# Attention and two expert layers on one core: the second low part of layer one moves from GpSimd to VectorE

## Chip, core and metric

One NeuronCore of a Trainium2 chip runs the whole program. The time is the device time of one execution in microseconds, lower is better; the number used is the median of several executions.

## What is computed

```
# decaying causal linear attention, blockwise: q, k, v [2, 8, 768, 64]
out[block] = ((q k^T) * Dmask) v + (q * lam_pow) kv_state
kv_state   = lam_block * kv_state + (k * rev_pow)^T v
# layer one: 1536 tokens x 512, one of 8 experts each (cosine logits, argmax)
out[mask] = gate * (relu(x[mask] @ w1[e]) @ w2[e])     # w1 [8, 512, 1024], w2 [8, 1024, 512]
# layer two: the same shapes, two of 8 experts each (noisy logits, top 2)
out[mask] += top2_w * (relu(x[mask] @ w1[e]) @ w2[e])
```

All of it is float32.

## The kernel before, in words

The attention runs first, in 12 tiles of 128 rows. Then the expert layers run as 18 **jobs**, one after the other: jobs 0 to 7 are the eight experts of layer one, with capacities of 224, 224, 224, 216, 208, 200, 192 and 184 tokens; jobs 8 to 17 belong to layer two. A job is 8 **steps**, one for each 128 hidden units, so there are 144 steps, numbered `s`. In a step TensorE makes the hidden units (`hstep`, tile `h` in PSUM) and, for the step two before (`LAG = 2`), the products with the second weight matrix (`ystep`, tiles `y`).

Float32 accuracy comes from splitting. `split(s)` is called three steps ahead (`LEAD = 3`) and cuts a weight tile into a high part in the format fp32r and a low part in bfloat16. For the first matrix ScalarE copies the high part `h1` (line 348) and VectorE subtracts to get the low part `l1` (line 350). For the second matrix ScalarE copies `h2` (line 349), and the low part `l2` (line 352) is subtracted by GpSimd or by VectorE, whichever the expression on line 352 chooses. Before, GpSimd does it as long as the job that step `s - 14` belongs to is one of layer one: for steps 0 to 77. From step 78 on VectorE does it. Steps 0 to 2 are split while the attention still runs. In 16 of the 144 steps nothing is split, so there are 128 `l2`.

The hidden units leave PSUM through ScalarE (`hs`, high part, line 778) and VectorE (`hs`, low part, line 779). Both engines work in order. So do the others, and the order of each is the order of the code: the dictionary `todo` says at which step which piece of the routing runs. The routing of layer two is computed job by job from the output of layer one (`gate_*`, `pe_0`, `pe_1`, `post1_*`, lines 840 to 1005): many small operations on VectorE, ScalarE and GpSimd, then gathers of token rows by GpSimd's DMA (line 693). Weights are reloaded by ScalarE's queue (lines 320 and 322); a reload waits until the subtractions have read the buffer.

Of the kernel before, what the change touches and what calls it, by code (L numbers as in the profile page):

```python
# [8 lines left out]
FT = mybir.dt.float32  # L9
# [20 lines left out]
NF = F // 128  # L30
# [25 lines left out]
LEAD = 3  # L56
# [8 lines left out]
XG6 = (6, 6, 6, 8, 8)  # L65
XG7 = (6, 6, 6, 7, 7)
C7 = (1, 1, 4)
POOL2 = 14
XP1 = (4, 6)
GATES = (-1, 1, 1, 2, 5, 6, 9)  # L70
GATES0 = (5, 5, 6, 7, 9, 8, 9)
# [28 lines left out]
def emit(ctx, tc, qt, kt, k, v, lam, moe_expert_emb, moe_tau, moe_w1, moe_w2, moe2_w_gate, moe2_w_noise,  # L100
         moe2_noise, moe2_w1, moe2_w2, out):
    nc = tc.nc
# [187 lines left out]
    JOBS = [Job(0, c, e=e) for e, c in enumerate(STAT1)]  # L290
# [37 lines left out]
    def drip(n=1):  # L328
        for _ in range(min(n, len(small))):
            fn, *a = small.pop(0)  # L330
            fn(*a)

    def split(s):
        if s >= NSTEP:
            return
        u, x = divmod(s, 4)
        r1, r2 = RAW[u]
        a1 = r1[:, :, x * 128:(x + 1) * 128]
        a2 = r2[:, x, :]
        if s % NF in JOBS[s // NF].raw:  # L340
            SPLIT[s] = (a1, None, a2, None)
            drip()
            return
        h1 = wts.tile([128, KD, 128], FR, name="h1", bufs=LEAD + 1)
        h2 = wts.tile([128, DM], FR, name="h2", bufs=LEAD + 2 + LAG)
        l1 = wts.tile([128, KD, 128], BF, name="l1", bufs=LEAD + 1)
        l2 = wts.tile([128, DM], BF, name="l2", bufs=LEAD + 2 + LAG)
        nc.scalar.activation(h1, a1, AF.Copy)  # L348
        nc.scalar.activation(h2, a2, AF.Copy)  # L349
        nc.vector.tensor_sub(l1, a1, h1.bitcast(FT))  # L350
        drip()
        (nc.gpsimd if not JOBS[max(0, s - POOL2) // NF].ly else nc.vector).tensor_sub(l2, a2, h2.bitcast(FT))  # L352
        SPLIT[s] = (h1, l1, h2, l2)


# [188 lines left out]
    for i in range(NTI + 1):  # L544
# [34 lines left out]
        if i in SPLITS:  # L579
            split(SPLITS.index(i))  # L580
# [53 lines left out]
    def parts(x):  # L634
        jb = JOBS[0]
        c = jb.c
        if not x:
# [6 lines left out]

    CALLS = {"E": early, "F": first_rows, "J": join, "P": parts, "O": O, "X": X, "R1": R1, "R2": R2,
             "RC": RC, "S": lambda i: split(len(SPLITS) + n - i), "W": lambda i: warm_up(WARM1[n - i], "px"), "R3": R3, "R4": R4}
    n = NTI - 1
    for calls in LATE:
# [583 lines left out]
    for u in range(3, 2 * NJ):  # L1232
        raw = [f % 4 for f in JOBS[(u - 3) // 2].raw if f // 4 == (u - 3) % 2]
        s = 4 * (u - 3) + max([WF] + [x + LAG for x in raw])
# [3 lines left out]
    for s in range(NSTEP + LAG):  # L1238
        j, f = divmod(s, NF)
        if s < NSTEP:  # L1240
            hstep(s)

        if s >= LAG and not (f == LAG and 0 < j <= E):
            if f == LAG + 1 and 0 < j <= E:
                ystep(s - LAG - 1)
            ystep(s - LAG)
        if f == LAG - 1 and j and not (j == NJ and JOBS[-1].row):
            ycopy(j - 1)
        for u in loads.get(s, ()):
            wload(u, nc.scalar)  # L1250
        if 12 <= s < 12 + 4 * 8 and s % 4 == 0:
            zero_out(s // 4 - 3)
        for fn, a in sorted(todo.get((j, f), ()), key=lambda x: (post1_e, pe_0, pe_1).index(x[0]) if x[0] in (post1_e, pe_0, pe_1) else 3):
            if fn in stages:
                drip(99)
            fn(*a)
        split(s + LEAD)
# [224 lines left out]
```

## Time and profile before

| | |
|---|---|
| median of 3 executions | 614.44 us (612.76 to 615.24) |
| the profiled execution | 615.32 us, span 613.6 us |
| TensorE matmul busy | 579.9 us, 95% of the span |
| VectorE busy | 395.1 us, 64% |
| ScalarE busy | 295.3 us, 48% |
| GpSimd busy | 303.2 us, 49% |
| granted TensorE clock, mean | 0.98 |

Busy means that an instruction of the engine is open in the trace, also while it waits inside for something. Matmuls are pipelined and their ends are modelled, so TensorE's busy share says little by itself; its idle times, and what ended them, say more. Attention takes the first 84 us, layer one from there to about 285 us, layer two the rest. All "us" in rows of the trace count from the start of the span.

### The profile page before, as it was taken

The numbers are of one execution on the slowest core, as the hardware profiler recorded it, in microseconds if no ns is written. First come the engines' busy times: TensorE is split into PE (matmuls) and PEld (weight loads), VectorE is DVE, ScalarE is ACT, GpSimd is POOL, SyncE is SP. The second block draws the span as 40 slices with busy tenths as digits, with TensorE's granted clock in tenths as the row PEclk, the third lists the DMA queues.
The fourth block names the chain that finished last, engine by engine and source line by source line (L and its number), as shares of the span: only waits on it lengthen the run. The fifth ranks groups of instructions, "written<-read, shape, count | busy, mean of one in ns | idle before, by whom it ended". The sixth has DMA issues, their size and how long they took to land.

```text
span 613.6 us, 11525 instructions
## 1 busy us (share of the span) xinstructions
PE 579.9 (95%) x4212; PEld 474.1 (77%) x4213; DVE 395.1 (64%) x1097; ACT 295.3 (48%) x689; POOL 303.2 (49%) x484
## 2 busy tenths in 40 slices
PE   5999889999988999998989999999999999999992
PEld 2898778888877888886766877777777898679761
DVE  3688847898898798898987447465664127323620
ACT  1466426776665667665444434344443135314410
POOL 5676547977867678776763500341303332412203
PEclk8899999999999999999999999999999999999996
DMA  7999546858866674675675732554526637737103
GB/s 202 342 332 391 226 131 208 300 201 297 285 222 242 235 268 173 232 251 173 207 212 209 226 139 63 126 196 154 107 93 171 209 71 234 257 138 189 18 5 56
DMA packets 59955, 119.52 MB, mean 195 GB/s; under 512 B 5469, under 2 KB 7045, under 8 KB 59890
## 3 DMA queue, kind: packets, MB, share of 16 engines
q10 hardware_dynamic: 37232, 73.74, 34.3%
q0 software_dynamic: 9376, 25.48, 16.3%
q1 hardware_dynamic: 13282, 19.48, 9.5%
q8 instruction: 35, 0.57, 0.4%
q14 instruction: 30, 0.25, 0.1%
HBM read 100.55 MB, written 18.14 MB: 193 GB/s over the span
## 4 chain that ended last, share of the span: by engine, by line
PE 79%; DVE 8%; POOL 4%; DMA 3%; issue 3%; ACT 1%; ACTq 0%; DVEq 0%; POOLq 0%
PE h L756 11%; PE h L757 10%; PE h L759 9%; PE y L759 7%; PE y L754 6%; PE y L757 4%; PE y L756 4%; PE t L732 3%; PE h L750 3%; PE y L750 3%; PE y L786 2%; PE y L787 2%; PE y L788 2%; PE po L410 2%; PE px L443 2%
## 5 line engine op out<-in xcount | busy, mean ns | idle before, releaser
L756 PE MATMUL h<-xs,h 128*128 128x224 f32 (+10 forms) x512 | 152.9, 322 | 4.2 <-DVE hs L779 4.2
L1050 POOL DMA_INDIRECT out_dram<-orow,ix x30 | 47.6, 1586 | 206.3 <-DVE orow L1048 153.0
L757 PE MATMUL h<-xs,h 128*128 128x224 f32 (+10 forms) x512 | 142.8, 302 | 0.3 <-DVE xs L737 0.3
L350 DVE TENSOR_TENSOR l<-r,h 128x512 bf16<-128x512 f32 x128 | 112.9, 882 | 35.3 <-ACT h L348 34.9
L352 POOL TENSOR_TENSOR l<-r,h 128x512 bf16<-128x512 f32 x78 | 103.6, 1336 | 15.5 <-ACT h L349 14.1
L759 PEld LDWEIGHTS <-l 128*128 128x128 bf16 x896 | 68.8, 97 | 45.5 <-issue 24.0
L778 ACT ACTIVATE hs<-h 128x224 fp32r<-128x224 f32 (+10 forms) x128 | 52.0, 406 | 105.5 <-PE h L759 97.0
L756 PEld LDWEIGHTS h<-xs,h 128*128 128x128 f32 x512 | 97.4, 190 | 6.9 <-DVE hs L779 5.1
L757 PEld LDWEIGHTS h<-xs,h 128*128 128x128 f32 x512 | 97.5, 190 | 1.8 <-DVE xs L737 1.0
L779 DVE SCALAR_TENSOR_TENSOR hs<-h,hs 128x224 fp32r<-128x224 f32 (+10 forms) x128 | 57.8, 452 | 54.0 <-ACT hs L778 53.0
L759 PE MATMUL h<-xs,l 128*128 128x224 bf16 (+10 forms) x512 | 87.4, 292 | 0.0
L348 ACT ACTIVATE h<-r 128x512 fp32r<-128x512 f32 x128 | 79.8, 623 | 9.9 <-POOL l L352 4.8
L349 ACT ACTIVATE h<-r 128x512 fp32r<-128x512 f32 x128 | 79.4, 621 | 0.0
L759 PE MATMUL y<-hs,l 128*128 128x224 bf16 (+8 forms) x384 | 70.3, 289 | 0.0
L754 PE MATMUL y<-hs,h 128*128 128x448 f32 (+5 forms) x256 | 68.0, 384 | 0.0
L737 DVE TENSOR_TENSOR xs<-t,xs 128x416 fp32r<-128x416 f32 (+7 forms) x42 | 24.6, 587 | 48.7 <-ACT xs L736 48.5
L756 PE MATMUL y<-hs,h 128*128 128x416 f32 (+2 forms) x128 | 51.2, 400 | 0.0
L736 ACT ACTIVATE xs<-t 128x416 fp32r<-128x416 f32 (+7 forms) x42 | 21.5, 516 | 53.5 <-PE t L732 48.2
L788 PE MATMUL y<-h,hs 128*128 128x512 f32 x80 | 46.6, 583 | 0.0
L757 PE MATMUL y<-hs,h 128*128 128x416 f32 (+2 forms) x128 | 44.7, 349 | 0.0
L754 PEld LDWEIGHTS y<-hs,h 128*128 128x128 f32 x256 | 44.0, 191 | 0.9
L693 POOL DMA_INDIRECT xw<-x,g x28 | 30.9, 1103 | 15.0 <-PE h L759 7.3
(274 smaller groups left out, 987.6 us busy)
## 6 DMA issues: line engine op xcount, KB each, us to landing
r<-in_moe_w_dram ACTq DMA_DIRECT2D x66, 1024.0 KB, 8.3
r<-in_moe_w_dram SPq DMA_DIRECT2D x6, 1024.0 KB, 9.1
x<-row POOLq DMA_DIRECT2D x8, 517.0 KB, 5.3
out_dram<-zeros ACTq DMA_DIRECT2D x7, 512.0 KB, 6.4
qt<-in_qt_dram SPq DMA_DIRECT2D x12, 256.0 KB, 5.8
kr<-in_k_dram SPq DMA_DIRECT2D x12, 256.0 KB, 7.9
vt<-in_v_dram SPq DMA_DIRECT2D x12, 256.0 KB
x<-xr POOLq DMA_DIRECT2D x11, 265.0 KB, 3.8
```

The lines of the kernel that those rows point to most:

```text
L348: nc.scalar.activation(h1, a1, AF.Copy)
L349: nc.scalar.activation(h2, a2, AF.Copy)
L350: nc.vector.tensor_sub(l1, a1, h1.bitcast(FT))
L352: (nc.gpsimd if not JOBS[max(0, s - POOL2) // NF].ly else nc.vector).tensor_sub(l2, a2, h2.bitcast(FT))
L754: nc.tensor.matmul(o[:, :2 * c], hi, mov, start=first, stop=False, skip_group_check=True)
L756: nc.tensor.matmul(o[:, :c], hi, mov[:, :c], start=first, stop=False, skip_group_check=True)
L757: nc.tensor.matmul(o[:, :c], hi, mov[:, c:], start=False, stop=False, skip_group_check=True)
L759: nc.tensor.matmul(o[:, :c], lo, upper_half(mov[:, :c]), start=False, stop=last, skip_group_check=True)
L778: nc.scalar.activation(hh, ph[:, :c], AF.Relu)
L779: nc.vector.scalar_tensor_tensor(hl, ph[:, :c], 0.0, hh.bitcast(FT), op0=OP.max, op1=OP.subtract)
L788: nc.tensor.matmul(PY[j][t], hl, h2, start=False, stop=f == NF - 1)
L1050: s = nc.gpsimd.indirect_dma_start(out=out[:, :], out_offset=bass.IndirectOffsetOnAxis(ap=ix[:p, t:t + 1], axis=0), in_=row[:p], in_offset ...
```

## The change

`l2` goes to GpSimd for the three steps that are split during the attention, and to VectorE for all others. The arithmetic, the buffers and the rest of the code stay as they are.

```
-POOL2 = 14
...
         nc.scalar.activation(h1, a1, AF.Copy)
         nc.scalar.activation(h2, a2, AF.Copy)
         nc.vector.tensor_sub(l1, a1, h1.bitcast(FT))
         drip()
-        (nc.gpsimd if not JOBS[max(0, s - POOL2) // NF].ly else nc.vector).tensor_sub(l2, a2, h2.bitcast(FT))
+        (nc.gpsimd if s < LEAD else nc.vector).tensor_sub(l2, a2, h2.bitcast(FT))
         SPLIT[s] = (h1, l1, h2, l2)
```

75 instructions move, one for each of the steps 3 to 77. A line was taken out at the top of the file, so that every later line has a number one lower after the change. TensorE's, ScalarE's and SyncE's instructions keep their order. The weights `l2` on TensorE and the weight reloads of ScalarE's queue now wait for VectorE where they waited for GpSimd.

On VectorE, the place is the fifth step of job 3, where the routing of an earlier job makes the tables `pa` and `pb`. Before:

```order
L993 TENSOR_TENSOR pa_2671<-iotap,r2s 128x512
L995 TENSOR_TENSOR ge_2601<-ge_2601 128x4x12
L996 TENSOR_TENSOR pb_2672<-oi_2605,ge_2601 128x384
L350 TENSOR_TENSOR l_2685<-r_2178,h_2683 128x512
L779 SCALAR_TENSOR_TENSOR hs<-h,hs 128x216
L737 TENSOR_TENSOR xs<-t,xs 128x2x208
L350 TENSOR_TENSOR l_2725<-r_2178,h_2723 128x512
L779 SCALAR_TENSOR_TENSOR hs<-h,hs 128x216
```

After the change, the same place:

```order
L992 TENSOR_TENSOR pa_2671<-iotap,r2s 128x512
L994 TENSOR_TENSOR ge_2601<-ge_2601 128x4x12
L995 TENSOR_TENSOR pb_2672<-oi_2605,ge_2601 128x384
L349 TENSOR_TENSOR l_2685<-r_2178,h_2683 128x512
L351 TENSOR_TENSOR l_2686<-r_2180,h_2684 128x512
L778 SCALAR_TENSOR_TENSOR hs<-h,hs 128x216
L736 TENSOR_TENSOR xs<-t,xs 128x2x208
L349 TENSOR_TENSOR l_2725<-r_2178,h_2723 128x512
L351 TENSOR_TENSOR l_2726<-r_2180,h_2724 128x512
L778 SCALAR_TENSOR_TENSOR hs<-h,hs 128x216
```

Each `l2` now stands between the `l1` of its split and the low part `hs` of the step that TensorE makes next. Nothing else moved on VectorE.

On GpSimd, the place is the first steps of layer one, right behind the gathers of jobs 1 and 0 (`ok` and `cid` say which gathered rows count and where they go, `meta` are the last columns of the gathered rows, `gq` the gate's numbers). Before:

```order
L665 TENSOR_TENSOR cid_1353<-ok_1352,sid_136 128x4
L352 TENSOR_TENSOR l_1401<-r_668,h_1399 128x512
L352 TENSOR_TENSOR l_1426<-r_942,h_1424 128x512
L716 COPY meta<-xw 128x18 x2
L352 TENSOR_TENSOR l_1469<-r_942,h_1467 128x512
L716 COPY meta<-xw 128x18 x2
L352 TENSOR_TENSOR l_1509<-r_942,h_1507 128x512
L352 TENSOR_TENSOR l_1552<-r_942,h_1550 128x512
L664 TENSOR_TENSOR ok_1352<-ok_1352,capm 128x12
```

After the change, the same place:

```order
L664 TENSOR_TENSOR cid_1353<-ok_1352,sid_136 128x4
L715 COPY meta<-xw 128x18 x4
L663 TENSOR_TENSOR ok_1352<-ok_1352,capm 128x12
L664 TENSOR_TENSOR cid_1353<-ok_1352,sid_136 128x12
L854 TENSOR_TENSOR gq<-gq,meta 128x2
```

Five `l2` are gone from this piece; the small operations of the routing that stood behind them follow one another. It is the same in the later steps up to 77.

## Rows read from the trace of the kernel before

**Rows 1.** The page, busy time of each engine over the span.

```profile
PE 579.9 (95%) x4212; PEld 474.1 (77%) x4213; DVE 395.1 (64%) x1097; ACT 295.3 (48%) x689; POOL 303.2 (49%) x484
```

**Rows 2.** Busy time by stretch: two jobs of layer one, then around 200 us.

```profile
core 0: us, PE busy (x) PEld busy (x) DVE busy (x) ACT busy (x) POOL busy (x), PEclk, DMA share, GB/s
111.10:135.10 24.00, 24.00 (x193) 20.52 (x191) 21.02 (x51) 17.43 (x47) 19.54 (x26) 1.00 0.76 265
...
256.00:281.20 25.20, 22.51 (x197) 19.94 (x195) 22.34 (x53) 16.43 (x43) 18.85 (x27) 1.00 0.61 210
...
198.00:201.00 3.00, 3.00 (x15) 2.54 (x15) 2.46 (x16) 0.54 (x2) 0.33 (x2) 0.50 0.52 109
201.00:204.00 3.00, 3.00 (x26) 2.79 (x26) 2.55 (x8) 2.70 (x7) 1.73 (x4) 0.98 1.05 401
```

**Rows 3.** Instructions in order of time on TensorE: its idle times, and what ended them.

```profile
95.40 0.37 PE L756 MATMUL h<-xs,h 128*128 128x224 f32 x1 [0.46 <-DVE hs L779]
...
171.54 0.37 PE L756 MATMUL h<-xs,h 128*128 128x216 f32 x1 [1.55 <-DVE hs L779]
...
196.31 0.37 PE L756 MATMUL h<-xs,h 128*128 128x208 f32 x1 [1.64 <-DVE hs L779]
...
262.08 0.66 PE L882 MATMUL t<-ident,yt 128*128 128x128 f32 x4 [0.92 <-DVE tab L1005]
...
281.24 1.13 PE L890 MATMUL t<-yt,wgn 128*32 128x256 f32 x6 [1.76 <-DVE yt L827]
...
307.58 0.34 PE L1004 MATMUL t<-pb,pa 128*128 128x96 f16 x4 [0.67 <-DVE pb L996]
...
308.51 0.39 PE L756 MATMUL h<-xs,h 128*128 128x256 f32 x1 [0.58 <-DVE hs L779]
...
311.00 0.47 PE L786 MATMUL y<-h,hs 128*128 128x512 f32 x1 [0.80 <-DVE orow L1048]
```

**Rows 4.** VectorE in order of time before the idle time at 171.54.

```profile
165.21 2.38 DVE L996 TENSOR_TENSOR pb<-oi,ge 128x384 f16<-128x384 f32 x1
167.52 3.68 DVE L350 TENSOR_TENSOR l<-r,h 128x512 bf16<-128x512 f32 x1
171.12 0.37 DVE L779 SCALAR_TENSOR_TENSOR hs<-h,hs 128x216 fp32r<-128x216 f32 x1
```

**Rows 5.** GpSimd in the same stretch.

```profile
165.87 1.30 POOL L352 TENSOR_TENSOR l<-r,h 128x512 bf16<-128x512 f32 x1
...
168.15 2.50 POOL L352 TENSOR_TENSOR l<-r,h 128x512 bf16<-128x512 f32 x2
```

**Rows 6.** Line 350 by stretch: layer one, then layer two; busy time and count.

```profile
85.00:325.00 240.00, 78.50 (x78) 0.99 0.67 231
325.00:590.00 265.00, 32.37 (x47) 1.00 0.50 150
```

**Rows 7.** The other groups of VectorE, 85 to 325 us: busy time, mean ns of one.

```profile
L996 DVE TENSOR_TENSOR pb<-oi,ge 128x384 f16<-128x384 f32 x8 | 10.8, 1356 | 0.8
...
L944 DVE TENSOR_TENSOR oh<-iota,row 128x16 f32<-128x16 f32 x16 | 8.0, 539 | 0.0
...
L862 DVE SCALAR_TENSOR_TENSOR gq<-gq 128x2 f32<-128x2 f32 x8 | 5.2, 647 | 0.3
L981 DVE SCALAR_TENSOR_TENSOR r2s<-r2s 128x4 f32<-128x4 f32 x8 | 5.0, 630 | 0.3
...
L861 DVE RECIPROCAL gq<-gq 128x2 f32<-128x2 f32 x8 | 1.3, 160 | 0.9 <-POOL gq L857 0.9
```

**Rows 8.** Line 996 alone: shortest, median and longest in ns.

```profile
L996 DVE TENSOR_TENSOR pb<-oi,ge x8: 558/1168/2381, 139.1 to 305.8; 128x384 f16<-128x384 f32 x8
```

**Rows 9.** A split in layer two, where VectorE makes both low parts.

```profile
378.00 0.69 DVE L350 TENSOR_TENSOR l<-r,h 128x512 bf16<-128x512 f32 x1 [1.06 <-ACT h L348]
378.61 0.69 DVE L352 TENSOR_TENSOR l<-r,h 128x512 bf16<-128x512 f32 x1
```

**Rows 10.** ScalarE in order of time at the start of layer one.

```profile
93.53 0.63 ACT L348 ACTIVATE h<-r 128x512 fp32r<-128x512 f32 x1 [4.80 <-POOL l L352]
```

**Rows 11.** The chain of work that ended last, before the idle time at 307.58.

```profile
304.22 1.48 DVE ge L995
...
305.80 1.72 DVE pb L996
```

More of the change, by code (lines that the diff above doesn't have):

```diff
@@ L67 @@
 C7 = (1, 1, 4)
-POOL2 = 14
 XP1 = (4, 6)
@@ L351, in split @@
         drip()
-        (nc.gpsimd if not JOBS[max(0, s - POOL2) // NF].ly else nc.vector).tensor_sub(l2, a2, h2.bitcast(FT))
+        (nc.gpsimd if s < LEAD else nc.vector).tensor_sub(l2, a2, h2.bitcast(FT))
         SPLIT[s] = (h1, l1, h2, l2)
```

## The prediction

> **What bounds the kernel now.** The first view is the page: TensorE is busy 95% of the span, VectorE 64% and the others less [rows 1]. So a gain can only come from times in which TensorE stands still, or runs at its lower clock, and I looked for those in layer one, the stretch that the change touches. The busy times by stretch show that a job of layer one takes some 24 us, in which VectorE is busy 21 to 22 us, an occupancy of 88% [rows 2]. VectorE is nearly full there, and the change gives it more work. That is the first thing to clear up.
>
> TensorE's instructions in order of time then show eight idle times in layer one and just behind it, all ended by VectorE [rows 3]: 0.46, 1.55, 1.64, 0.92, 1.76, 0.67, 0.58 and 0.80 us, together 8.38 us. What is VectorE doing before them? Ahead of the second one it runs `pb` for 2.38 us and an `l1` for 3.68 us [rows 4]. Neither is normally that long: the shortest `pb` is 0.56 us [rows 8], and in layer two 47 instructions of line 350 take 32.37 us, 0.689 us each [rows 6]. In the same moments GpSimd runs `l2`: one that lies inside the `pb`, two in a row that lie inside the `l1` [rows 5]. The `l1` ends only after the second of them. The reader should see that VectorE is not working there. It is open and held up, and its occupancy of 88% is partly that.
>
> **What the change takes from VectorE.** I count the held-up time by groups. In layer one line 350 takes 78.5 us for 78 instructions [rows 6]; at 0.689 us each they would take 53.7, so 24.8 us are delay. Line 996 takes 10.8 us for 8; at its shortest it would take 4.5, so 6.3 us [rows 7, 8]. Lines 944, 862 and 981 work on 2 to 16 columns and take 8.0, 5.2 and 5.0 us for 16, 8 and 8 [rows 7]; a reciprocal of the same size takes 0.16 us [rows 7], so they should take 2.6, 1.3 and 1.3, and 13.0 us are delay. That makes 44.1 us from five groups, and more from others that I leave out. After the change no `l2` runs on GpSimd in this stretch, so this goes.
>
> **What it adds to VectorE.** 75 instructions. In layer two one `l2` follows its `l1` 0.61 us after that one's start [rows 9], and that is the price of an added instruction in a full queue: 75 x 0.61 = 45.8 us. So VectorE's load stays about where it is, 44.1 less against 45.8 more, or a little less with the groups left out. What changes is the shape: before, the delays came in lumps of 1 to 3 us in one place; after, 0.61 us is added evenly in each step of about 3 us. TensorE needs the low part of `hs` two steps later, so it can bear 0.6 us and cannot bear 3.
>
> `l2` waits for ScalarE's `h2`, which follows `h1` by about 0.5 us; the `l1` before it hides that at 0.61 us. If `l1` were shorter, VectorE would wait the difference, below 0.1 us, with `hs` behind it.
>
> **What it takes from GpSimd.** 75 instructions from an engine whose other work in layer one is small operations and gathers. These no longer queue behind `l2`. One such wait went through ScalarE: at the start of layer one a weight reload waits for the first `l2`, which stands behind four gathers, and ScalarE stands still for 4.80 us [rows 10] until that `l2` is done. This leads to TensorE's 0.46 us [rows 3]. After the change VectorE makes that `l2` right behind its `l1`, before the gathers are through.
>
> **A rule, and what it would make of this.** The Trainium skill, Perfetto Trace Analysis, section Optimizing Scalar/DVE Operations, says that a saturated VectorE can be relieved by giving work to ScalarE or even GpSimd, and warns that VectorE and GpSimd share a read port, so that moving work between the two might not help. The first half speaks against this change, since VectorE is the fuller engine; the price that it would have is that of the first rival below. The second half is what the rows of layer one look like, where the held-up instructions read two tensors each from SBUF and end with GpSimd's `l2`; by that half the 44.1 us come back.
>
> **The sum.** Taken back: TensorE's eight idle times, 8.38 us. Also the clock: from 198 to 201 us the granted clock is 0.50, the lower of the two levels, right behind the idle time at 196.31; 15 matmuls ran in these 3 us against 26 in the next 3 [rows 2], so 3 x (1 - 15/26) = 1.3 us were lost. Without the idle times before it I expect the clock to stay up. Together 9.7 us. Against it: the last three idle times, 2.05 us together, lie in a chain on VectorE in which `ge` and `pb` were held up (1.48 us and 1.72 us [rows 11], some 2.4 us of that delay), but into which three `l2` come, 1.8 us. There I leave half of the idle time standing, 1.0 us. At the other places up to 3 us of delay go for one or two `l2`, so their idle time goes as a whole. The change is worth 9.7 - 1.0 = 8.7 us. The profiled execution took 615.3 us, 0.9 above the median: 615.3 - 8.7 = 606.6, and 605.7 from the median; I say 606.5.
>
> Bounds: at best all 9.7 us come back and the median is taken, 604.7; small gaps between matmuls, which I did not count, could bring 2 to 3 more: 602. At worst the waits shift to a next cause and almost nothing comes back.
>
> **Rivals.**
> - *VectorE is the bound, slower.* If the delays on VectorE had another cause than `l2` on GpSimd (its gathers or its small operations), they would stay, and 8 x 0.61 = 4.9 us would be added to 21 us in each job: 25.9 us where a job now takes 24 to 25. That is some 1.5 us for each 8 steps, and 75 steps are 9.4 times that, some 14 us: 629. Against it: the 47 instructions of layer two take 0.689 us each though GpSimd still gathers and scatters there [rows 6]. Chance 0.06.
> - *`hs` comes late in each step, slower.* In VectorE's order each `l2` stands in front of an `hs` that TensorE needs. If TensorE waited 0.3 us for it in each of the 75 steps, 22 us would be lost against 8.7 gained: 628. It decides from 8.7 / 75 = 0.12 us in a step upward. For it: occupancy stays near 88%. Against it: two steps of slack, and no stretch of TensorE's idle time behind a single delay under 1 us. Chance 0.08.
> - *The stalls move, no change.* TensorE's idle times are 1.4% of the span. Behind VectorE the gathers of the next job's rows or the chain of small operations could be next, and take the same places: a gain of 0 to 3 us, 613. Chance 0.12.
> - *The forecast*, 602 to 611: 0.74.
>
> A measurement of this kernel tells 0.5%, 3.1 us, from no change. Faster by more than that: 0.74; within: 0.12; slower: 0.14. The range of 8 in 10 reaches from 602 into the third rival, to 613.5.
>
> **What would show it.** Right: line 350 (349 after) near 0.69 us in layer one, none of VectorE's small operations over 1 us, VectorE's busy time in a job still at 20 to 22 us, GpSimd's down by some 10; no idle time of TensorE over 1 us at the steps where `pb` is made; no stretch at clock 0.50 near 200 us; ScalarE's wait of 4.80 us gone. Wrong: line 350 still over 0.9 us on average (first rival), or many short idle times of TensorE that end with `hs`, or matmuls of `y` started late (second). The prediction fails most simply if the idle times vanish from where they are and an equal sum appears elsewhere, between 281 and 325 us above all, where VectorE's own chain is longest.

## The result and the profile after

The changed kernel took 607.24 us against 614.01 us of the kernel before on the same chip: a ratio of 0.9889, 95% interval 0.986 to 0.9919, 6.8 us faster. This is the median of six executions; a seventh took 713.81 us at a mean granted clock of 0.747 and is left out (with it the median is 607.94 us). Run twice more beside the kernel before, further down, it took 603.13 us against 614.06 (ratio 0.9817, 0.9781 to 0.9853) and 604.17 us against 612.50 (0.9878, 0.9838 to 0.9917).

Busy time by engine over the span, from the page of the changed kernel:

```profile
PE 582.1 (96%) x4212; PEld 477.7 (79%) x4213; DVE 378.5 (62%) x1172; ACT 295.0 (48%) x689; POOL 213.1 (35%) x409
```

Against [rows 1], VectorE has 75 instructions more and 16.6 us less. GpSimd has lost 90.1 us. Where the time came from, and where a part of it went, busy times by stage show: the first 30 us, the rest of the attention, layer one up to the logits of its last job, and everything behind. First the kernel before, then the changed one. After the length of a stretch stand the busy times of TensorE, its weight loads, VectorE, ScalarE and GpSimd, then the granted clock.

```profile
0.00:30.00 30.00, 22.38 (x209) 15.95 (x212) 13.92 (x51) 8.74 (x22) 17.75 (x65) 0.89 0.89 269
30.00:84.00 54.00, 49.86 (x605) 44.13 (x601) 42.34 (x199) 28.90 (x74) 32.68 (x62) 1.00 0.81 290
84.00:281.20 197.20, 190.56 (x1568) 166.16 (x1566) 167.81 (x426) 130.26 (x337) 151.95 (x219) 0.99 0.67 233
281.20:613.60 332.40, 317.14 (x1837) 247.89 (x1837) 171.06 (x424) 127.38 (x257) 100.85 (x140) 0.99 0.51 150
```

```profile
0.00:30.00 30.00, 21.41 (x151) 15.34 (x154) 10.69 (x36) 6.14 (x15) 14.49 (x60) 0.66 0.86 263
30.00:88.70 58.70, 55.32 (x660) 48.96 (x656) 45.67 (x212) 31.39 (x81) 35.95 (x65) 0.97 0.77 270
88.70:276.20 187.50, 186.97 (x1568) 164.34 (x1568) 155.71 (x491) 130.13 (x337) 73.20 (x154) 1.00 0.70 245
276.20:608.30 332.10, 318.44 (x1837) 249.02 (x1837) 166.45 (x434) 127.34 (x257) 89.49 (x130) 0.98 0.52 150
```

Layer one is 9.7 us shorter, 197.20 to 187.50 us, and TensorE is idle there for 0.53 us where it was idle for 6.64. But layer one starts 4.7 us later. The attention before it has the same instructions in the same order; in this execution its first 30 us ran at a granted clock of 0.66 against 0.89. So the 5.2 us between the two profiled executions (615.32 and 610.09 us) hide much of what layer one gained. Behind layer one this execution gained 0.3 us only; TensorE's clock was at the lower level again for a part of the stretch from 317 to 324 us (0.76 granted):

```profile
317.00:324.00 7.00, 6.47 (x29) 4.66 (x29) 2.83 (x5) 2.46 (x5) 4.68 (x8) 0.76 0.97 373
```

VectorE at the place of [rows 4], in order of time:

```profile
167.75 0.56 DVE L995 TENSOR_TENSOR pb<-oi,ge 128x384 f16<-128x384 f32 x1
168.60 0.69 DVE L349 TENSOR_TENSOR l<-r,h 128x512 bf16<-128x512 f32 x1 [0.29 <-ACT h L347]
169.21 0.68 DVE L351 TENSOR_TENSOR l<-r,h 128x512 bf16<-128x512 f32 x1
169.81 0.38 DVE L778 SCALAR_TENSOR_TENSOR hs<-h,hs 128x216 fp32r<-128x216 f32 x1
```

`pb`, `l1`, `l2` and `hs` are through in 2.44 us; before, `pb` and `l1` alone took 6.0. By groups, the answer to [rows 7] (columns as there), and line 349 in layer one, the answer to [rows 6]:

```profile
L995 DVE TENSOR_TENSOR pb<-oi,ge 128x384 f16<-128x384 f32 x8 | 4.5, 559 | 0.8
...
L943 DVE TENSOR_TENSOR oh<-iota,row 128x16 f32<-128x16 f32 x16 | 2.0, 166 | 0.0
...
L980 DVE SCALAR_TENSOR_TENSOR r2s<-r2s 128x4 f32<-128x4 f32 x8 | 1.3, 162 | 0.3
L861 DVE SCALAR_TENSOR_TENSOR gq<-gq 128x2 f32<-128x2 f32 x8 | 1.3, 160 | 0.3
```

```profile
88.00:322.00 234.00, 54.30 (x79) 0.99 0.71 244
```

Each group is at its undisturbed length: line 349 takes 0.687 us on average against 1.006. Of VectorE's instructions from the start of layer one to 311 us, 42 took more than 1 us before; at the same place none does now. Of the eight idle times of [rows 3], one has left a rest:

```profile
276.22 1.39 PE L889 MATMUL t<-yt,wgn 128*32 128x256 f32 x8 [0.55 <-DVE yt L826]
```

ScalarE's wait of [rows 10] is down from 4.80 to 0.65 us, and VectorE's memset ends it:

```profile
94.00 0.64 ACT L347 ACTIVATE h<-r 128x512 fp32r<-128x512 f32 x1 [0.65 <-DVE yt L1255]
```

### The profile page after: what moved, and what is told of

It is laid out like the page before. It is cut to its first block, busy times and chain, and to the rows that moved or that the text cites. A ratio compares the mean times of both kernels' runs of the same rounds, so it can differ in the third digit from the quotient of the medians.

```text
span 608.3 us, 11489 instructions
## 1 busy us (share of the span) xinstructions
PE 582.1 (96%) x4212; PEld 477.7 (79%) x4213; DVE 378.5 (62%) x1172; ACT 295.0 (48%) x689; POOL 213.1 (35%) x409
## 4 chain that ended last, share of the span: by engine, by line
PE 87%; DVE 4%; DMA 3%; POOL 2%; issue 1%; ACT 0%; POOLq 0%; DVEq 0%
PE h L755 12%; PE h L756 11%; PE h L758 10%; PE y L753 8%; PE y L758 8%; PE y L756 4%; PE y L755 4%; PE t L731 4%; PE h L749 3%; PE y L749 3%; PE y L785 2%; PE y L786 2%; PE y L787 2%; PE po L409 2%; PE pa L387 2%; PE px L442 2%
## 5 line engine op out<-in xcount | busy, mean ns | idle before, releaser
L349 DVE TENSOR_TENSOR l<-r,h 128x512 bf16<-128x512 f32 x128 | 88.0, 688 | 35.6 <-ACT h L347 34.7
L351 DVE TENSOR_TENSOR l<-r,h 128x512 bf16<-128x512 f32 x125 | 85.4, 683 | 0.0
```

What stands on the lines that cost most here:

```text
L351: (nc.gpsimd if s < LEAD else nc.vector).tensor_sub(l2, a2, h2.bitcast(FT))
```

## The experiments

All are edits of the changed kernel, with the line numbers of the kernel before, or a few more where lines are added. Each was timed in 5 rounds beside the kernel before. The first four ran on one chip, where that took 613.94 us; the next four on a second, 614.06; the one with all `l2` on VectorE on a third, 613.47; the last two on the second again, 612.50.

### A dummy subtraction on GpSimd beside the l2 on VectorE

```
         (nc.gpsimd if s < LEAD else nc.vector).tensor_sub(l2, a2, h2.bitcast(FT))
+        if LEAD <= s < 78:
+            nc.gpsimd.tensor_sub(dummy, zeros[:, :DM], h2.bitcast(FT))
```

> The changed kernel, and beside each l2 of steps 3 to 77 on VectorE a dummy subtraction of the same size on GpSimd, at the place in its order where l2 was (it reads h2 and a constant tile and writes a tile that nothing reads; no weight reload waits for it). Theory (VectorE is held up while GpSimd subtracts): line 350 goes back to about 1.0 us on average in layer one, VectorE needs over 24 us in a job, the idle times of TensorE return and are more than before: 618 to 632 us. Rival (the gain came from GpSimd's queue, whose small operations and reloads no longer wait): the small operations wait again, about the time before, 612 to 615 us. If neither counts: 606 to 609 us.

Measured: 648.81 us, ratio 1.0584 (1.0563 to 1.0605). The direction is the theory's, the size is over its range. Busy time by stretch, two jobs of layer one, and VectorE's groups there:

```profile
140.70:168.70 28.00, 25.12 (x196) 20.90 (x196) 26.50 (x64) 16.37 (x42) 20.46 (x28) 1.00 0.65 227
168.70:195.90 27.20, 24.41 (x196) 20.94 (x197) 26.49 (x64) 16.31 (x42) 20.95 (x28) 1.00 0.69 235
```

```profile
L353 DVE TENSOR_TENSOR l<-r,h 128x512 bf16<-128x512 f32 x69 | 66.1, 958 | 0.0
L351 DVE TENSOR_TENSOR l<-r,h 128x512 bf16<-128x512 f32 x69 | 64.3, 931 | 5.1 <-ACT h L349 4.7 <-issue 0.3
```

VectorE is busy 26.5 of 27.2 to 28.0 us in a job: it has become the bound. Its busy time over the span is 445.8 us against 378.5, so the 75 dummies, whose results nobody reads, cost it 67.3 us, 0.90 us each.

### A memset of the same length in place of the dummy subtraction

```
+        if LEAD <= s < 78:
+            nc.gpsimd.memset(dummy, 0.0)          # dummy: [128, 1344] float32
```

> The changed kernel, and on GpSimd, at the place where l2 was, a memset of 1344 columns of float32 in each of the steps 3 to 77: about as long as an l2 (estimate 1.3 us, from 0.61 us for 512 and 0.29 us for 128 columns in the trace of before), but it reads nothing. Theory (VectorE is held up by GpSimd's reading instructions): VectorE's line 350 stays at 0.69 us and the time at 605 to 609 us. If any long GpSimd instruction holds VectorE up: 615 us and more, as with the dummy subtraction. Rival (GpSimd's queue): the small operations of the routing wait as before, 611 to 615 us with line 350 at 0.69 us.

Measured: 604.99 us, ratio 0.9851 (0.9832 to 0.9869). GpSimd is as full as before (299.1 us busy, [rows 1] has 303.2), with instructions nearly as long, from the groups of GpSimd and of VectorE in layer one:

```profile
L355 POOL MEMSET dummy<- 128x1344 f32 x75 | 91.7, 1223 | 2.1
```

```profile
L351 DVE TENSOR_TENSOR l<-r,h 128x512 bf16<-128x512 f32 x81 | 56.0, 691 | 10.4 <-ACT h L349 9.7 <-issue 0.3
```

VectorE's line takes 0.691 us: not held up. At one place the filled queue does reach TensorE: VectorE waits 1.47 us for `meta` (0.88 in the second run of the changed kernel), and TensorE's idle time behind it is 1.11 us (0.54 there).

```profile
269.15 0.16 DVE L1028 SCALAR_TENSOR_TENSOR ws<-meta 128x2 f32<-128x2 f32 x1 [1.47 <-POOL meta L719]
...
272.25 1.39 PE L893 MATMUL t<-yt,wgn 128*32 128x256 f32 x8 [1.11 <-DVE yt L830]
```

That is 0.6 us. So GpSimd's queue, as far as the memsets fill it, did not cost the time. They do not fill it in every way: an `l2` on GpSimd also waited there for ScalarE's `h2`, 14.1 us in all in the kernel before, and a memset waits for nothing.

```profile
L352 POOL TENSOR_TENSOR l<-r,h 128x512 bf16<-128x512 f32 x78 | 103.6, 1336 | 15.5 <-ACT h L349 14.1
```

Of the two kinds of GpSimd instruction tried, the one that reads two tensors holds VectorE up and the one that only writes does not; one that reads a single tensor was not tried.

### No l2 in steps 3 to 77

```
+        if LEAD <= s < 78:
+            l2 = l1.rearrange("p k c -> p (k c)")
+        else:
             (nc.gpsimd if s < LEAD else nc.vector).tensor_sub(l2, a2, h2.bitcast(FT))
```

The buffers of `l1` go from 4 to 7, since `ystep` now reads them too.

> The changed kernel without the l2 of steps 3 to 77: TensorE takes l1's numbers in place of l2, so its matmuls stay and the second product of these steps is another one. VectorE saves 75 x 0.61 = 45.8 us. Theory (in the changed kernel VectorE's load no longer reaches TensorE): within 1.5 us of the changed kernel, 605 to 609 us. Rival (each l2 still delays hs by 0.6 us, and TensorE waits a part of it): 3 to 6 us faster than the changed kernel.

Measured: 605.95 us, ratio 0.9859 (0.9826 to 0.9893). VectorE's busy time falls by 39.4 us to 339.1 (0.53 us for each `l2`, less than the 0.61 assumed), and the time by nothing that can be told: the changed kernel's ratios are 0.9817 to 0.9889. By stage, layer one:

```profile
87.60:274.50 186.90, 186.85 (x1568) 164.35 (x1568) 122.72 (x431) 129.76 (x336) 58.59 (x155) 1.00 0.70 246
```

186.9 us against 187.5 and 187.9 in the two runs of the changed kernel shown here, and TensorE without a pause. The added work is free to within 1 us in layer one.

### l2 behind hs in VectorE's order

```
-        (nc.gpsimd if s < LEAD else nc.vector).tensor_sub(l2, a2, h2.bitcast(FT))
+        sub = lambda: (nc.gpsimd if s < LEAD else nc.vector).tensor_sub(l2, a2, h2.bitcast(FT))
+        if LEAD <= s < 78:
+            later.append(sub)
+        else:
+            sub()
...
         nc.vector.scalar_tensor_tensor(hl, ph[:, :c], 0.0, hh.bitcast(FT), op0=OP.max, op1=OP.subtract)
+        while later:
+            later.pop(0)()
         drip()
```

> The changed kernel, with each l2 of steps 3 to 77 put behind the next low part of hs in VectorE's order instead of in front of it. Theory: TensorE does not wait for hs in the changed kernel, so the time is the same within 1.5 us. Rival (hs comes late in each step): 2 to 6 us faster, with VectorE's busy time the same.

Measured: 605.61 us, ratio 0.9875 (0.9856 to 0.9894), layer one 187.6 us in the trace. The order makes no difference that can be told; `hs` does not come late.

### The change in two parts, by steps, and every other step

```
-        (nc.gpsimd if s < LEAD else nc.vector).tensor_sub(...)
+        (nc.gpsimd if s < 64 else nc.vector).tensor_sub(...)                          # only 64 to 77
+        (nc.gpsimd if s < LEAD or 64 <= s < 78 else nc.vector).tensor_sub(...)        # only 3 to 63
+        (nc.gpsimd if s < LEAD or s < 78 and s % 2 else nc.vector).tensor_sub(...)    # every other
```

> Only the l2 of steps 64 to 77 go to VectorE; those of steps 0 to 63 stay on GpSimd. Theory (the gain is TensorE's idle times, where they lie): the three idle times from 307 to 311 us and perhaps the one at 281 shrink, 2 to 3.5 us gained, 610.5 to 612.5 us. Rival (in this stretch VectorE's own chain is longest, and l2 in it costs what it frees): 613 to 615 us.

Measured: 610.32 us, ratio 0.993 (0.9901 to 0.9959), 3.7 us.

> Only the l2 of steps 3 to 63 go to VectorE; those of steps 64 to 77 stay on GpSimd. Theory: the idle times at 95, 171, 196 and 262 us go with the stretch at the lower clock, 5 to 7 us gained, 607 to 609 us. Rival (the last steps carry half of the gain or more): 610 us and more.

Measured: 606.54 us, ratio 0.9887 (0.9844 to 0.993), 7.5 us. Together 11.2 us; the whole change beside them gave 10.9. TensorE's instructions in order of time, those in layer one and just behind it with idle times of over 0.4 us that VectorE ended, first with only 64 to 77 moved, then with only 3 to 63 moved:

```profile
95.78 0.37 PE L756 MATMUL h<-xs,h 128*128 128x224 f32 x1 [0.45 <-DVE hs L779]
...
174.48 0.37 PE L756 MATMUL h<-xs,h 128*128 128x216 f32 x1 [0.81 <-DVE hs L779]
...
201.59 0.36 PE L757 MATMUL h<-xs,h 128*128 128x200 f32 x1 [0.89 <-DVE xs L737]
...
260.72 0.66 PE L882 MATMUL t<-ident,yt 128*128 128x128 f32 x4 [1.25 <-DVE tab L1005]
```

```profile
271.20 1.39 PE L890 MATMUL t<-yt,wgn 128*32 128x256 f32 x8 [1.61 <-DVE yt L827]
...
297.53 0.34 PE L1004 MATMUL t<-pb,pa 128*128 128x96 f16 x4 [0.80 <-DVE pb L996]
...
298.46 0.38 PE L756 MATMUL h<-xs,h 128*128 128x256 f32 x1 [0.58 <-DVE hs L779]
...
300.94 0.47 PE L786 MATMUL y<-h,hs 128*128 128x512 f32 x1 [0.82 <-DVE orow L1048]
```

Each kernel keeps idle times where GpSimd still subtracts, and is free of those of [rows 3] where it does not. This is the closest that the runs come to seeing cause and place at once. The places are not the same to the last one, though: with only 64 to 77 moved, the idle time at 171 us is half as long, that at 196 us is gone, and one of 0.89 us stands at 201.59 us. From the first idle time to the one at line 882 it takes 164.9 us, 166.7 us in [rows 3], and in this stretch both kernels have the same `l2` on GpSimd. So 1.7 us of what the trace of before shows there comes and goes with the execution. Neither of these two profiled executions has a stretch at the lower clock near 200 us, the first one although GpSimd subtracts there; that stretch is not shown to belong to the `l2`.

> Of the steps 3 to 77, the l2 of odd ones stay on GpSimd and those of even ones go to VectorE. Theory (VectorE is held up for as long as GpSimd subtracts, and added work comes on top): delay and added work each half; no two l2 in a row on GpSimd, so no delay over 1.4 us, and TensorE's idle times are mostly gone: 606 to 610 us. Rival (the gain is in proportion to the number of l2 moved): 610 us. VectorE's line 350 near 0.85 us on average in layer one.

Measured: 606.71 us, ratio 0.9885 (0.9847 to 0.9922). Line 350 in layer one:

```profile
85.00:325.00 240.00, 60.79 (x80) 1.00 0.70 242
```

0.76 us on average, below the 0.85 expected, and 7.4 us gained with half of the instructions. Its idle times near 300 us remain, up to 1.02 us. The rival's 610 us is outside the interval, which ends at 609.3; but half of the 10.9 us that the whole change gains on this chip would be 608.6 us, and that is inside. So this run does not settle whether TensorE feels the long delays alone or the sum of all.

### The changed kernel again

> The changed kernel again, on the same chip as these, to size it: TensorE's clock in the attention, which the change does not touch, was at the lower level for 20 us in the profiled execution of the changed kernel and for 7 us in that of the kernel before. If that is chance, the median lies at 605 to 607 us and the clock's stretch differs from execution to execution; if it belongs to the changed kernel, the median is 607 to 609 us again.

Measured: 603.13 us (602.44 to 603.77). By stage:

```profile
0.00:30.00 30.00, 21.24 (x219) 15.65 (x220) 14.56 (x53) 9.28 (x23) 18.09 (x66) 0.89 0.85 251
30.00:83.40 53.40, 49.21 (x592) 43.48 (x588) 41.72 (x196) 28.36 (x73) 32.33 (x59) 1.00 0.83 303
83.40:271.30 187.90, 187.22 (x1568) 164.46 (x1568) 154.92 (x491) 129.97 (x337) 73.21 (x154) 1.00 0.70 244
271.30:601.80 330.50, 316.91 (x1837) 247.96 (x1837) 166.27 (x434) 127.36 (x257) 89.50 (x130) 0.98 0.52 151
```

The attention now has the clock and the length that the kernel before has (0.89 in the first 30 us, 83.4 us), layer one stays at 187.9. The run of the changed kernel further down has the same (0.89, 83.7 us). So the late start of layer one in the first comparison came with the clock of the attention and not with the change. The median is even below the range expected for chance. Over the span, the mean granted clock was 0.984 to 0.989 in these executions, and 0.969 to 0.987 in the six of the first comparison. Executions of the same mean clock can be compared over all chips: at 0.984 nine of the kernel before took 613.50 to 614.26 us, and four of the changed kernel 603.72 to 604.19, some 10 us less.

### All l2 on VectorE, and the first three after the attention

```
-        (nc.gpsimd if s < LEAD else nc.vector).tensor_sub(l2, a2, h2.bitcast(FT))
+        nc.vector.tensor_sub(l2, a2, h2.bitcast(FT))
```

> Also the l2 of steps 0 to 2, which are split during the attention, go to VectorE. Theory: each of them frees some 0.5 us there (the operation of line 474 takes 0.70 us beside a GpSimd subtraction and 0.18 us without one) and costs 0.61 us: no change against the changed kernel run last, 602 to 604.5 us. If VectorE's order in the attention reaches TensorE: 1 to 2 us slower, 604 to 606 us.

Measured: 608.09 us, ratio 0.9891 (0.9852 to 0.993), 5.4 us gained instead of 8 to 11, and above both ranges. The changed kernel was not run on this chip; its stages can be compared, since the attention ran at the same granted clock as in the second run. By stage, the attention:

```profile
0.00:30.00 30.00, 21.99 (x207) 15.76 (x210) 13.80 (x49) 8.61 (x22) 17.52 (x64) 0.89 0.84 246
30.00:86.70 56.70, 49.92 (x603) 44.16 (x601) 45.09 (x202) 29.06 (x74) 29.95 (x59) 1.00 0.80 288
```

It is 3.3 us longer than the 83.4 us above. VectorE and GpSimd in it, in order of time:

```profile
56.56 2.12 DVE L352 TENSOR_TENSOR l<-r,h 128x512 bf16<-128x512 f32 x1
...
64.40 1.19 DVE L474 TENSOR_TENSOR oh<-iota8u,mi 128x8 bf16<-128x8 uint32 x1
```

```profile
56.83 1.28 POOL L363 TENSOR_TENSOR qD<-qt,qpat 128x512 f32<-128x512 f32 x1
```

The first `l2` is now itself held up, by GpSimd's multiplication for the attention. The other two take 0.69 us each; behind the second one the operation of line 474 takes 1.19 us in place of the 0.70 it took beside an `l2` on GpSimd. TensorE waits 1.39, 1.21 and 0.64 us for line 474 behind the three of them; in the second run of the changed kernel only the third of these waits is there, 0.57 us. The same instruction that is free in layer one is not free here: in the attention VectorE's chain is the one that TensorE waits for.

The last edit makes these three on VectorE after the attention, just before the gathered rows of job 0 are split:

```
-        (nc.gpsimd if s < LEAD else nc.vector).tensor_sub(l2, a2, h2.bitcast(FT))
+        sub = lambda: nc.vector.tensor_sub(l2, a2, h2.bitcast(FT))
+        if s < LEAD:
+            later.append(sub)
+        else:
+            sub()
...
     for calls in LATE:
+        while later and calls is LATE[-1]:
+            later.pop(0)()
```

> The changed kernel, with the l2 of steps 0 to 2 on VectorE too, but made after the attention, where VectorE waits for a gather, and not inside it. Theory: in the attention neither does GpSimd hold VectorE up with them (0.5 us each) nor do they stand in VectorE's order, so layer one starts up to 1.5 us earlier than in the changed kernel: 0.5 to 1.5 us faster than it on the same chip, about 602 us. If other GpSimd work falls into the same place of VectorE's order and holds it up instead: no change.

Measured: 604.59 us, ratio 0.9866 (0.9833 to 0.9899).

> The changed kernel beside it, on the same chip, to compare: 602 to 606 us; how much of it is the clock in the attention.

Measured: 604.17 us. No difference between the two, so the 0.5 to 1.5 us expected did not come. The place that `l2` left is taken, as VectorE and then GpSimd show:

```profile
65.11 1.80 DVE L478 TENSOR_TENSOR oh<-iota8u,mi 128x8 bf16<-128x8 uint32 x1
```

```profile
65.61 1.27 POOL L367 TENSOR_TENSOR qD<-qt,qpat 128x512 f32<-128x512 f32 x1
```

No version tried is faster than the changed kernel.

## Why the prediction was right, and where its sizes were off

**What bounds the kernel.** Right. VectorE's occupancy was partly waiting inside instructions; with the `l2` gone from GpSimd it fell although work was added. The trace of before shows it over all of layer one: of the 73 `l1` from 84 to 311 us, the 26 that overlap with a GpSimd `l2` by more than 0.1 us take 1.58 us on average, the other 47 0.68 us. The dummy subtraction brings the delays back, the memset does not.

**What the change takes from VectorE: too small.** The five groups gave 44.1 us, and I left the others out. The whole is 395.1 + 45.8 - 378.5 = 62.4 us, 0.83 us for each `l2` that GpSimd made; with the 39.4 us that leaving the `l2` out saved in place of the 45.8, it is 56.0 us and 0.75. This is why VectorE is busy 18 to 20 us in a job (18.15 and 17.96 us in the jobs that answer to [rows 2], 19.6 to 20.0 in those between, from the second run) where I expected 20 to 22, and why the dummy subtraction cost more than expected: I had put too low a price on a GpSimd subtraction.

**What it adds.** 0.5 to 0.6 us each, hidden by TensorE's work. Shown by leaving the `l2` out (186.9 against 187.5 and 187.9 us in layer one) and by moving it behind `hs`.

**The sum: 8.7 us expected; 6.8, 10.9 and 8.3 us measured.** It was too small; at the same mean clock the gain is some 10 us. In the traces layer one is 9.3 to 9.7 us shorter (197.2 to 187.9 and 187.5), where the sum has 7.6: five idle times, 6.3 us, and the clock, 1.3 us. The idle times gave 6.0 to 6.1 us. The other 3.3 to 3.6 us are matmuls, the same 1568, that are open for less time (190.56 to 187.22 and 186.97 us). Taking off 1.3 us for the clock leaves some 2 us. I had named small gaps of 2 to 3 us in the bounds and left them out of the sum; whether these 2 us are such gaps, the runs do not show. Nor is the clock's 1.3 us shown to be the change's, as the run with only 64 to 77 moved tells. Behind layer one I left 1.0 us standing between 307 and 311 us, and nothing of it is left. The delay of `ge` and `pb`, 2.4 us, was more than the 1.8 us that the `l2` added, and the idle times are not proportional to what is left over. That stage is 1.9 us shorter in the second run.

The spread of the measured gains is not in the change. The times of the executions follow the mean granted clock, and in the two profiled executions of the changed kernel shown here it differs in the attention for the most part. I had not put that into the range as a term of its own. So it is partly luck that the first comparison came out so near to the 606.5 us: a gain larger than the sum, and a clock that took a part of it back.

**ScalarE's reload, and GpSimd's queue.** The wait of 4.80 us went as said, and it was worth the 0.46 us of TensorE and no more: with every other step on GpSimd, step 3 among them, TensorE is idle for 0.47 us at that place again. GpSimd's shorter queue is worth some 0.6 us, at the last logits of layer one, by the memset.

**The rivals.** VectorE as the bound is what the dummy subtraction shows: it needs GpSimd's reading and VectorE's added work together. `hs` late in each step is refuted. The stalls did not move on; TensorE is idle for 0.5 to 0.7 us in all of layer one. What did turn up between 281 and 325 us, in the first of the two profiled executions, is a stretch at the lower clock, and the stage was 1.6 us longer there than in the second.

**The rule on offloading** (the Trainium skill, Perfetto Trace Analysis, Optimizing Scalar/DVE Operations) speaks by its first half for leaving the `l2` on GpSimd. That did not hold here: taking work off GpSimd and giving it to the fuller VectorE made VectorE less busy by 16.6 us. Its warning on the shared port is what the runs agree with.

## What to carry to other kernels

An engine's busy time is not its work: compare each group with the same instruction in a stretch where the other engine is quiet, before deciding that the engine is full. A GpSimd instruction that reads two tensors can cost VectorE more than doing that work itself (0.75 to 0.83 us held up against 0.5 to 0.6 us of work here), and in lumps. Moving it costs nothing only where VectorE's chain has slack to TensorE; the same three instructions in the attention cost some 3 us.

## What the runs showed of the hardware

- The delay depends on what GpSimd does, not on how long: 75 subtractions of about 1.3 us cost VectorE 0.90 us each, 75 memsets of 1.22 us left line 351 at 0.691 us.
- It also depends on where VectorE reads. The low part of `hs` reads one tensor from PSUM and one from SBUF. Of the 24 at 224 columns in the kernel before, four lie wholly inside a GpSimd `l2`, as the one below; they take 0.379 to 0.392 us, and those that touch no `l2` 0.376 to 0.392. The Trainium skill, GPSIMD Engine Reference, section Key points, names VectorE instructions with two SBUF inputs as those in contention with GpSimd; these rows agree.

```profile
97.91 1.29 POOL L352 TENSOR_TENSOR l<-r,h 128x512 bf16<-128x512 f32 x1
...
97.96 0.39 DVE L779 SCALAR_TENSOR_TENSOR hs<-h,hs 128x224 fp32r<-128x224 f32 x1
```

- TensorE's clock in the attention is at its lower level for a time that differs from execution to execution: the first 30 us had 0.66 and 0.89 granted for the same kernel. This alone moved the start of layer one by some 5 us, where the change gains 7 to 11.
